# A gated mix of linear attention and a squared-ReLU MLP: TensorE's order written by hand, operands of 448 columns moved to another place in their 256 bytes

## The chip, the cores and the metric

The kernel runs on one core of a Trainium2 chip. The metric is the device time of one launch in microseconds. All matrix products take float32 data in the float32r form, and most numbers are split in two parts (`h` and `l`, for high and low), so that one logical product of two split operands is three matmuls: high by high, high by low, low by high.

## What is computed

```python
x = A_x                                       # 2048 x 448, float32
g = sigmoid((x * gate_w).sum(-1))             # one gate for each row
# a: linear attention, 16 heads of 28
q, k, v = split(x @ A_wqkv)
phi = lambda t: where(t > 0, t + 1, exp(t)) + 1e-6
kv  = einsum("hsd,hse->hde", phi(k), v);  z = phi(k).sum over s
o   = (phi(q) @ kv) / (phi(q) . z + 1e-6)
a   = o @ A_wo
# b: MLP, 448 -> 1792 -> 448
b   = relu(x @ B_w1 + B_b1) ** 2 @ B_w2 + B_b2
return g * a + (1 - g) * b
```

## The kernel before

The 2048 rows are cut into four blocks `b` of 512 columns of the transposed `x` (`xt`), and each block into four tiles `t` of 128 rows. The 448 input features are four chunks `c`; the last one is packed so that two matmuls do for it, and a product over all features is 11 matmuls (3 + 3 + 3 + 2). The 1792 hidden features are 14 slices `f` of 128.

`up(b, f)` makes one hidden slice: 11 matmuls with moving operands of 512 columns into `h_ps` (line 213), then ReLU and square on ScalarE (lines 217, 218) and the split on VectorE (`hh`, `hl`; lines 62, 65). `down(b, f)` multiplies it with `w2` into four accumulators `o_ps`: 12 matmuls whose moving operand has 448 columns (line 242). `keys(t)` is 11 matmuls with the key weights `wk_s` as moving operand. In this kernel that operand has 450 columns: the two last ones carry the gate's weights, and a one-column copy (line 280) takes the gate's logit out of `k_ps`. `gram(b, c)` accumulates phi(k) by x (`g_ps`, 12 matmuls of 448 columns, 8 for the last chunk).

There are two stages. In the first, each block does hidden slices 0 to 6, its keys and its gram. In the second, the blocks come in the order 3, 0, 1, 2 (`order`; `n` counts the place in it, `fl` the slice in the half) and do slices 7 to 13, the queries (`q_ps`, 11 matmuls of 512 columns, 7 for `c == 3`), the denominators (`d_ps`), the scaling of the queries (`scaled`: `qh`, `ql`) and the attention (`a_ps`, 11 matmuls of 448 columns for a tile). `finish` joins the two results and stores a tile.

At the seam between the stages stands the product of kv with the output weights. `kv_product` (`kv_ps`, line 364) is followed by four `m_product(j)`, of three matmuls each, into `m_ps`. Each result is split into the tile `m`, of which there is one buffer (`tag="m", bufs=1`), and spread over the partitions of `m_s` by five DMAs that GpSimd issues (lines 398 to 400). `m_ps` shares two PSUM buffers (`ms_p`, tag `ms`) with `k_ps`, `g_ps`, `q_ps`, `d_ps` and `a_ps`, in the order in which the source asks for them.

A planner (`TileContext`) orders the instructions of every engine by its own estimates: the order of the source is a priority, and TensorE's blocks may be cut into each other. Around the slices 9 and 10 of a block in the second stage, for instance, it laid the matmuls of `a_ps`, `h_ps` and `o_ps` between each other. Semaphores keep the data right whatever the order; each engine runs its own list strictly in order.

Matmul operands lie in SBUF at addresses that the pools assign. In this kernel's program the moving operands of 512 columns begin at a multiple of 256 bytes in their partition, those of 448 and 450 columns at 64 modulo 256, but for the 12 of `m_ps`, which begin at 0 modulo 256. Small unused ends of tiles (`warm`, `side`, `off`, `wkm`, the 16 columns behind `w1`) set these places.

At the start, `load_w1(0, 0, c)` and `load_x(0, c)` alternate on SyncE's queue, with the first x chunk in two halves; 18 warm-up matmuls on zeros run meanwhile, and `up_chunk` then works chunk by chunk over four hidden slices.

Of the kernel before, what the change touches and what calls it, by code (L numbers as in the profile page):

```python
# [15 lines left out]
P = 128  # L16
# [14 lines left out]
def gated_mix_kernel(ctx: ExitStack, tc: tile.TileContext, xt, xn, wk, wq, wv, wo, w1a, w1b, w2, b1, b2, hmask,  # L31
# [4 lines left out]
    keep = ctx.enter_context(tc.tile_pool(name="keep", bufs=1))  # L36

# [59 lines left out]
    def load_x(b, c, a=0, z=TB):  # L97
        if a == 0:
            x_raw[b, c] = slot([P, TB], F, f"xr{b}_{c}")
        load(x_raw[b, c][:, a:z], xt[b, c][:, a:z])  # L100

    def split_x(b, c, a=0, z=TB):
        if c == 0 and a == 0:
            xs[b] = (keep.tile([P, 4, TB], R, name=f"xh{b}", tag="xh", bufs=2),
                     keep.tile([P, 4, TB], R, name=f"xl{b}", tag="xl", bufs=2))
        (xh, xl), r = xs[b], x_raw[b, c]
        if c < 3:
            split_hi(act, xh[:, c, a:z], r[:, a:z])
            split_lo(dve, xl[:, c, a:z], r[:, a:z], xh[:, c, a:z])
        else:  # L110
            split_last(xh[:, 3, a:z], xl[:, 3, a:z], r[:, a:z], side)
# [11 lines left out]
    def load_w1(h, g, c):  # L123
        w1_raw[h, g, c] = slot([P, (TB, 3 * P)[g]], F, f"w1r{h}{g}{c}")
        load(w1_raw[h, g, c], (w1a, w1b)[g][h, c])

    def split_w1(h, g, c, hi_eng=act):
        if c == 0:
            n = (TB, 3 * P)[g]
            w = keep.tile([P, 7 * n + (16, 0)[g]], R, name=f"w1_{h}{g}", tag=f"w1{g}", bufs=1)  # L130
            w1_s[h, g] = w[:, :7 * n].rearrange("p (c n) -> p c n", c=7)
        split_w(w1_s[h, g], c, w1_raw.pop((h, g, c)), hi_eng, dve)
# [20 lines left out]
    def load_wk(c):  # L153
        wk_raw[c] = slot([P, D + 2], F, f"wkr{c}")
        load(wk_raw[c], wk[c])
# [4 lines left out]
    warm = keep.tile([P, 400], mybir.dt.bfloat16, name="warm")[:, :256]  # L160
    dve.memset(warm, 0.0)
    warm_ps = acc_p.tile([P, 512], F, name="warm_ps", tag="acc")
    for _ in range(18):
        pe.matmul(warm_ps[:, :256], warm[:, :P], warm, start=True, stop=True)
# [6 lines left out]
    for c in range(4):  # L171
        load_w1(0, 0, c)
        if c == 0:
            load_x(0, c, 0, TB // 2)
            load_x(0, c, TB // 2, TB)
        else:
            load_x(0, c)
# [12 lines left out]
    b2_s = keep.tile([P, D], F, name="b2_s")  # L190
    hm = keep.tile([P, P], R, name="hm")
    dve.memset(ones, 1.0)
    ksum = keep.tile([P, D], F, name="ksum")
    part = [keep.tile([P, D], F, name=f"part{t}") for t in range(NT)]
# [8 lines left out]
    def up_chunk(ps, b, f, c):  # L203
# [8 lines left out]
        for n, (a, m) in enumerate(terms):  # L212
            pe.matmul(ps, a, m, start=(c == 0 and n == 0), stop=(c == 3 and n == 1))  # L213

    def hidden(ps, b, f):
        r = slot([P, TB], F, f"hr{b}_{f}")
        act.activation(r, ps, AF.Relu, bias=b1_s[:, f:f + 1])  # L217
        act.activation(r, r, AF.Square)  # L218
        h = slot([P, TB], R, f"hh{b}_{f}")
        lo = slot([P, TB], R, f"hl{b}_{f}")  # L220
        split_hi(dve, h, r)
        split_lo(dve, lo, r, h)
        hs[f] = (h, lo)

    def up(b, f):
# [3 lines left out]
        hidden(ps, b, f)  # L229
# [34 lines left out]
    def keys(t):  # L264
        b, i = divmod(t, 4)
        ps = ms_p.tile([P, 512], F, name=f"k_ps{t}", tag="ms")
        products(ps[:, :D + 2], [term for c in range(4)
                                 for term in terms_x(*xs[b], slice(i * P, (i + 1) * P), wk_s, slice(0, D + 2), c)])
# [6 lines left out]
        if t == 0:  # L275
            pool.memset(tmp_p.tile([P, 48], F, name="off"), 0.0)

        def after():
            phi(ps[:, :D], e, r, p)
            dve.tensor_copy(logit[:, t:t + 1], ps[:, D:D + 1])  # L280
# [8 lines left out]
            raw = xn_raw.pop(t)  # L289
            split_hi(act, nh[:, :D], raw)  # L290
# [22 lines left out]
    wq_s = keep.tile([P, 7, TB], R, name="wq_s")  # L313
# [72 lines left out]
    def m_product(j):  # L386
# [5 lines left out]
        def after():  # L392
# [4 lines left out]
            for c in range(3):  # L397
                pool.dma_start(out=m_s[p:p + 32, c::4, :D][:, :2], in_=m[c * 32:c * 32 + 32])
            pool.dma_start(out=m_s[p:p + 16, 3, :D], in_=m[96:112, 0])
            pool.dma_start(out=m_s[p + 16:p + 32, 3, :D], in_=m[112:, 1])  # L400
# [67 lines left out]
    def attention(b, i):  # L468
# [4 lines left out]
        for c in range(3):  # L473
            h, lo = qs[c]
            terms += [(h[:, cols], m_s[:, c, :D]), (h[:, cols], m_s[:, 4 + c, :D]), (lo[:, cols], m_s[:, c, :D])]
        h, lo = qs[3]
        terms += [(h[:, cols], m_s[:, 3, :D]), (lo[:, cols], m_s[:, 3, :D])]
# [4 lines left out]

    todo = []
# [10 lines left out]
    for c in range(4):  # L494
        if c == 0:
            split_x(0, 0, 0, TB // 2)
            split_w1(0, 0, 0, hi_eng=dve)
            split_x(0, 0, TB // 2, TB)
# [3 lines left out]
        for f in range(4):  # L502
            up_chunk(first[f], 0, f, c)
    for f in range(2):
        hidden(first[f], 0, f)
# [5 lines left out]
    wkm = keep.tile([P, 3632], R, name="wk_s", tag="wkm", bufs=1)  # L511
    wk_s = wkm[:, :7 * TB].rearrange("p (c n) -> p c n", c=7)
# [4 lines left out]
    for c in range(4):  # L517
        split_w(wk_s[:, :, :D + 2], c, wk_raw[c], act, dve)
# [5 lines left out]
    split_w2(2)  # L524
    load(b2_s, b2.partition_broadcast(P))
# [31 lines left out]
    todo += gram(0, 0)  # L557
    split_x(1, 2)
    down(0, 5)
    run_todo()  # L560
    todo += gram(0, 1)
    split_x(1, 3)

    for b in range(1, NB):
        for f in range(NH):
            run_todo()
            up(b, f)
            if f == 0:
                down(b - 1, NH - 1)
                half_done(b - 1)  # L570
                if b == 1:
                    todo += gram(0, 2)
                    run_todo()
                    todo += gram(0, 3)
                    run_todo()
# [48 lines left out]
    for n, b in enumerate(order):  # L624
        then = order[n + 1] if n + 1 < NB else None
        for f in range(NF - NH, NF):
            fl = f - NH
            run_todo()
            up(b, f)
# [6 lines left out]
            else:  # L636
                down(order[n - 1], NF - 1)
                for i in range(4):
# [113 lines left out]
```

## Time and profile before

| | us |
|---|---|
| median of 3 runs | 442.17 (442.09 to 443.4) |
| the profiled execution | 441.92 |
| its span, first to last instruction | 440.1 |
| TensorE busy | 432.9 |
| VectorE busy | 268.0 |
| ScalarE busy | 172.7 |
| GpSimd busy | 58.5 |

The span is the time between the first and the last instruction that the profiler saw; the execution's own time is 1.8 us longer. A busy TensorE is one with a matmul in flight: the matmuls of a row overlap, so the time that a matmul costs is read from the distance of two starts, not from its length. Times in the rows are microseconds from the start of the span. In a row of the timeline the bracket is the idle time before it and what ended it.

### The profile page before, as it was taken

Reading aid. Unit: us, or ns where it says so; the run is one execution under the profiler, and the core shown is the slowest. Engines: PE = TensorE matmul, PEld = TensorE weight load, DVE = VectorE, ACT = ScalarE, POOL = GpSimd, SP = SyncE. Lnnn points to the kernel's source line nnn. Section 1 sums busy time; section 2 is a strip of 40 time slices with the busy share of each in tenths; the row PEclk is TensorE's granted clock in tenths of the full one; section 3 lists DMA queues with packets and bytes.
Section 4 is the critical chain, followed back from the end, with each engine's and each line's share of the span. In section 5 each row is a group of like instructions: output and inputs, shape, how many; then the busy total and the mean of one; then the engine's idle time right before and its main releaser. Section 6 shows DMA issues by size and latency. Waiting matters only on the chain.

```text
span 440.1 us, 5482 instructions
## 1 busy us (share of the span) xinstructions
PE 432.9 (98%) x2054; PEld 380.7 (87%) x2054; DVE 268.0 (61%) x452; ACT 172.7 (39%) x298; POOL 58.5 (13%) x76
## 2 busy tenths in 40 slices
PE   9999999999999999999999989999999999999996
PEld 6798898899888889898988868888888898888895
DVE  5958436552587427573467668788454984549423
ACT  5955235331355114451344334335322453234321
POOL 0233124210252005420002420000000000000000
PEclk9999999999999999999999999999999999999999
DMA  7652201021031210333146311040100501002002
GB/s 264 188 174 69 89 13 57 24 66 47 24 118 31 67 45 1 110 102 82 54 123 151 73 38 24 1 147 33 25 0 0 181 0 26 0 0 85 1 1 83
DMA packets 18315, 28.77 MB, mean 65 GB/s; under 512 B 2880, under 2 KB 12784, under 8 KB 18288
## 3 DMA queue, kind: packets, MB, share of 16 engines
q1 hardware_dynamic: 17072, 26.81, 19.9%
q0 software_dynamic: 1216, 1.61, 1.9%
q8 instruction: 16, 0.26, 0.3%
q14 instruction: 11, 0.09, 0.1%
HBM read 22.09 MB, written 3.67 MB: 59 GB/s over the span
## 4 chain that ended last, share of the span: by engine, by line
PE 91%; DVE 3%; DMA 2%; ACT 2%; issue 1%; SPq 0%; DVEq 0%; ACTq 0%
PE o_ps L242 30%; PE h_ps L213 28%; PE q_ps L77 8%; PE a_ps L77 8%; PE g_ps L77 8%; PE k_ps L77 7%; DMA wkr<-in_wk 1%; DMA xr<-in_xt 1%; PE kv_ps L364 1%; ACT hr L217 1%; PE m_ps L77 1%; DVE wk_s L65 0%; DVE hh L62 0%; DVE r L261 0%; DVE r L262 0%
## 5 line engine op out<-in xcount | busy, mean ns | idle before, releaser
L213 PE MATMUL h_ps<-xh,w 128*128 128x512 f32 x392 | 126.9, 392 | 0.1
L242 PE MATMUL o_ps<-w,hh 128*128 128x448 f32 x448 | 125.5, 363 | 0.7 <-DVE hh L62 0.7
L242 PEld LDWEIGHTS o_ps<-w,hh 128*128 128x128 f32 x448 | 83.8, 188 | 10.2 <-DVE hh L62 1.4
L213 PE MATMUL h_ps<-xl,w 128*128 128x512 f32 x224 | 87.5, 391 | 0.0
L213 PEld LDWEIGHTS h_ps<-xh,w 128*128 128x128 f32 x392 | 73.5, 188 | 15.4 <-ACT xh L58 0.4
L242 PE MATMUL o_ps<-w,hl 128*128 128x448 f32 x224 | 79.6, 363 | 0.0
L217 ACT ACTIVATE hr<-h_ps,b_s 128x512 f32<-128x512 f32 x56 | 38.3, 683 | 96.9 <-PE h_ps L213 89.8
L62 DVE CAST hh<-hr 128x512 fp32r<-128x512 f32 x56 | 25.3, 452 | 40.4 <-ACT hr L218 40.0
L213 PEld LDWEIGHTS h_ps<-xl,w 128*128 128x128 f32 x224 | 42.1, 188 | 8.3 <-DVE xl L65 0.4
L242 PEld LDWEIGHTS o_ps<-w,hl 128*128 128x128 f32 x224 | 42.0, 188 | 2.9 <-DVE hl L65 0.2
L65 DVE TENSOR_TENSOR hl<-hr,hh 128x512 fp32r<-128x512 f32 x56 | 41.1, 734 | 2.2
L218 ACT ACTIVATE hr<-hr 128x512 f32<-128x512 f32 x56 | 35.3, 630 | 1.3
L77 PE MATMUL k_ps<-wk_s,xh 128*128 128x450 f32 x112 | 33.7, 367 | 0.0
L77 PE MATMUL q_ps<-xh,wq_s 128*128 128x512 f32 x100 | 33.0, 390 | 0.0
L77 PE MATMUL a_ps<-m_s,qh 128*128 128x448 f32 x112 | 32.2, 362 | 0.0
L65 POOL TENSOR_TENSOR nl<-xnr,nh 128x384 fp32r<-128x384 f32 x16 | 18.2, 1139 | 94.2 <-ACT nh L58 94.2
L286 POOL TENSOR_TENSOR ksum<-ksum,r 128x448 f32<-128x448 f32 x15 | 19.3, 1284 | 52.1 <-DVE r L262 52.1
L481 DVE SCALAR_TENSOR_TENSOR part<-part,gate,u 128x448 f32<-128x448 f32 x16 | 10.9, 683 | 24.9 <-ACT u L480 24.9
L480 ACT ACTIVATE u<-a_ps,gate 128x448 f32<-128x448 f32 x16 | 10.2, 635 | 37.2 <-PE a_ps L77 37.2
L261 DVE TENSOR_SCALAR r<-k_ps 128x448 f32<-128x448 f32 x16 | 10.0, 623 | 23.7 <-ACT e L260 21.7
L77 PE MATMUL k_ps<-wk_s,xl 128*128 128x450 f32 x64 | 23.6, 369 | 0.0
L77 PE MATMUL g_ps<-pl,nh 128*128 128x448 f32 x64 | 23.3, 364 | 0.3 <-DVE pl L65 0.3
(104 smaller groups left out, 562.0 us busy)
## 6 DMA issues: line engine op xcount, KB each, us to landing
xr<-in_xt SPq DMA_DIRECT2D x27, 256.0 KB, 3.2
xnr<-in_xn SPq DMA_DIRECT2D x16, 224.0 KB, 2.6
out<-out SPq DMA_DIRECT2D x16, 224.0 KB, 2.0
w2r<-in_w SPq DMA_DIRECT2D x14, 224.0 KB, 2.9
w1r<-in_w1a SPq DMA_DIRECT2D x8, 256.0 KB, 2.8
w1r<-in_w1b SPq DMA_DIRECT2D x8, 192.0 KB, 2.9
m_s<-m POOLq DMA_DIRECT2D x12, 112.0 KB, 2.7
wqr<-in_wq SPq DMA_DIRECT2D x4, 256.0 KB, 3.0
```

Source lines behind the costliest of these rows:

```text
L62: eng.tensor_copy(hi, src)
L65: eng.tensor_tensor(lo, src, f32(hi), op=ALU.subtract)
L77: pe.matmul(out_ps, a, b, start=(i == 0), stop=(i == n - 1))
L213: pe.matmul(ps, a, m, start=(c == 0 and n == 0), stop=(c == 3 and n == 1))
L217: act.activation(r, ps, AF.Relu, bias=b1_s[:, f:f + 1])
L218: act.activation(r, r, AF.Square)
L242: pe.matmul(o_ps[i][:, :D], a, m, start=(f % NH == 0 and n == 0), stop=(f % NH == NH - 1 and n == 2))
L261: dve.tensor_scalar(r, ps, 0.0, 1e-6, op0=ALU.max, op1=ALU.add)
L286: pool.tensor_tensor(ksum, ksum, p, op=ALU.add)
L364: pe.matmul(kv_ps[:JE, js], wv_s[c][:, js], gsum[c][:, js], start=(c == 0), stop=(c == 3))
L480: act.activation(u, ps[:, :D], AF.Copy, scale=gate[:, 0, t:t + 1])
L481: dve.scalar_tensor_tensor(part[t], part[t], gate[:, 1, t:t + 1], u, op0=ALU.mult, op1=ALU.add)
```

## The change

TensorE is put under `tc.manual_schedule`: its instructions stand in the order of the source, uncut. The planner goes on ordering the other engines. The source was rearranged for that at the seam (`m_product`, `split_wo`), at `gram` of block 0, at the attention of the first block of the second stage, and at the end. The attention of the other three blocks keeps its place: tile `i` at slice `fl == i + 2`.

```diff
+    ctx.enter_context(tc.manual_schedule(engines={pe.engine}))
     todo = []
...
     split_x(1, 1)
     split_w2(6)
-    todo += gram(0, 0)
     split_x(1, 2)
     down(0, 5)
-    run_todo()
-    todo += gram(0, 1)
+    todo += gram(0, 0)
     split_x(1, 3)
...
             run_todo()
-            up(b, f)
+            if n == 0 and fl in (1, 2):
+                split_wo(2 * fl - 2)
+                split_wo(2 * fl - 1)
+            up(b, f, 2 if then is None and f == NF - 1 else 1)
+            if n == 0 and fl in (1, 2):
+                todo += m_product(2 * fl - 2)
+                run_todo()
...
             else:
                 down(order[n - 1], NF - 1)
                 for i in range(4):
+                    if n == 1:
+                        attention(order[0], i)
                     finish(order[n - 1], i)
             if n == 0:
+                if fl in (1, 2):
+                    todo += m_product(2 * fl - 1)
+                    run_todo()
                 if fl < 4:
                     todo += queries(b, (3, 0, 1, 2)[fl])
...
-                if fl in (1, 2):
-                    for j in range(2 * fl - 2, 2 * fl):
-                        split_wo(j)
-                        todo += m_product(j)
...
-                if fl == 6:
-                    for i in range(4):
-                        attention(b, i)
...
     last = order[-1]
+    down(last, NF - 2, range(3))
     for i in range(4):
-        for f in (NF - 2, NF - 1):
-            down(last, f, [i])
+        if i == 3:
+            down(last, NF - 2, [i])
+        down(last, NF - 1, [i])
         finish(last, i)
```

In the built program TensorE's blocks then follow each other like this, at the seam and in the second block after it (11 `q_ps` matmuls are 7 for `q3_3`):

```
q3_3 kv h3_8 m0 d3_7 m1 q3_0 h3_9 m2 d3_8 m3 q3_1 h3_10 d3_9 q3_2 h3_11 d3_10 den3 h3_12 d3_11 ...
q1_2 h1_7 d0_13 den1 h1_8 d1_7 h1_9 d1_8 a4 h1_10 d1_9 a5 q2_3 h1_11 ...
```

(`h3_8` is `up(3, 8)`, `d3_7` is `down(3, 7)`, `den3` is `denominators(3)`, `a4` is the attention of tile 4.)

The places of the 448-column moving operands change from 64 to 160 modulo 256: 1,200 matmuls of `o_ps`, `a_ps`, `g_ps` and `k_ps`. Those of 512 columns and those of `m_ps` stay where they were, and so do the stationary operands, but for the mask of the denominators. The pads that do this (`w1`, `wq_s`, `off`, `warm` laid into `part[0]`, `wk_s` and `m_s` as plain tiles of 7 x 448):

```diff
+    def new_w1(h, g):
+        n, a, z = ((TB, 0, 40), (3 * P, 24, 0))[g]
+        w = keep.tile([P, a + 7 * n + z], R, name=f"w1_{h}{g}", tag=f"w1{g}", bufs=1)
...
-    wkm = keep.tile([P, 3632], R, name="wk_s", tag="wkm", bufs=1)
-    wk_s = wkm[:, :7 * TB].rearrange("p (c n) -> p c n", c=7)
+    wk_s = keep.tile([P, 7, D], R, name="wk_s", tag="wkm", bufs=1)
```

The keys have 448 columns, and the logit comes from a VectorE instruction over the row tile of x and a broadcast gate weight `gw_s`, which is one more DMA of 224 KB on SyncE's queue (source line behind `split_w2(2)`; in the built program it stands behind the key weights, ahead of `b2_s`):

```diff
-        products(ps[:, :D + 2], ...)
+        products(ps[:, :D], ...)
...
-            dve.tensor_copy(logit[:, t:t + 1], ps[:, D:D + 1])
...
+            dve.scalar_tensor_tensor(e, raw, 1.0, gw_s, op0=ALU.mult, op1=ALU.mult, accum_out=logit[:, t:t + 1])
```

At the start x is loaded ahead of w1, chunk by chunk; the first w1 chunk comes in halves instead of the first x chunk; there are 15 warm-up matmuls instead of 18; and the first chunk's 12 matmuls go term by term over the four slices instead of slice by slice. Slice 0 of block 0 and the very last hidden slice go through ReLU, square and split in two halves of 256 columns (`parts=2`):

```diff
     for c in range(4):
-        load_w1(0, 0, c)
+        load_x(0, c)
         if c == 0:
-            load_x(0, c, 0, TB // 2)
-            load_x(0, c, TB // 2, TB)
+            load_w1(0, 0, c, 0, TB // 2)
+            load_w1(0, 0, c, TB // 2, TB)
...
+        if c == 0:
+            for n in range(3):
+                for f in range(4):
+                    up_chunk(first[f], 0, f, c, n)
...
-    for f in range(2):
-        hidden(first[f], 0, f)
+    hidden(first[0], 0, 0, 2)
+    hidden(first[1], 0, 1)
```

In the built program VectorE takes the low part of the first w1 chunk ahead of the low part of the first x chunk.

133 lines of the change are left out of this document (73 added, 60 removed).

## The prediction

> **What bounds the kernel now.** First the page: who is busy, and the chain of work that ended last.
>
> ```profile
> span 440.1 us, 5482 instructions
> PE 432.9 (98%) x2054; PEld 380.7 (87%) x2054; DVE 268.0 (61%) x452; ACT 172.7 (39%) x298; POOL 58.5 (13%) x76
> ...
> PE 91%; DVE 3%; DMA 2%; ACT 2%; issue 1%; SPq 0%; DVEq 0%; ACTq 0%
> ```
>
> TensorE (PE) is the bound. So a change pays only if it makes matmuls closer to each other or closes a gap between them, and every new wait of TensorE is paid in full. The view of busy time by stretches says where gaps are:
>
> ```profile
> 50.00:216.00 166.00, 166.00 (x797) 148.82 (x796) 87.12 (x145) 58.15 (x104) 36.23 (x39) 1.00 0.20 59
> 262.00:436.00 174.00, 174.00 (x819) 153.25 (x818) 113.44 (x187) 63.11 (x102) 0.45 (x1) 1.00 0.11 35
> ```
>
> The second number is TensorE's busy time, the next ones those of its weight loads, VectorE, ScalarE and GpSimd: TensorE is without a gap from 50 to 216 and from 262 to 436. An order of one's own has nothing to win there; it can only lose. What there is to win stands in these rows of the timeline, with the wait in the bracket:
>
> ```profile
> 16.16 1.08 PE L242 MATMUL o_ps<-w,hh 128*128 128x448 f32 x4 [0.75 <-DVE hh L62]
> ...
> 47.44 0.48 PE L77 MATMUL g_ps<-ph,nh 128*128 128x448 f32 x1 [0.18 <-ACT ph L58]
> ...
> 48.60 0.47 PE L77 MATMUL g_ps<-pl,nh 128*128 128x448 f32 x1 [0.28 <-DVE pl L65]
> ...
> 258.44 0.50 PE L77 MATMUL d_ps<-dh,hm 128*128 128x512 f32 x1 [1.32 <-ACT dh L58]
> ...
> 259.36 0.39 PE L77 MATMUL d_ps<-dl,hm 128*128 128x512 f32 x1
> ```
>
> A bracket is short of the loss, because a matmul counts as busy for some 0.15 us after the next could start, and the matmul after a wait takes another 0.11. So the losses are 0.75 + 0.26 = 1.0 at 16, 0.18 + 0.28 + 0.52 = 1.0 at 47 to 49, and at 258 1.32 + 0.15 and the 0.92 from 258.44 to 259.36, in which only two matmuls of 0.23 start: 1.9.
>
> What a matmul costs comes from the chain of waits, whose pieces are (start, length, how many):
>
> ```profile
> 19.05 2.26 PE k_ps L77 x11
> ...
> 236.07 0.63 PE m_ps L77 x3
> ...
> 252.34 2.53 PE q_ps L77 x11
> ...
> 270.96 8.80 PE a_ps L77 x44
> 279.76 4.99 PE q_ps L77 x22
> ```
>
> `k_ps` (450 columns) takes 2.26 / 11 = 0.2055 us, `a_ps` (448 columns, 64 modulo 256) 8.80 / 44 = 0.200, and so do `o_ps` and `g_ps`, `m_ps` (448 columns, 0 modulo 256) 0.63 / 3 = 0.21, `q_ps` (512 columns, 0 modulo 256) 4.99 / 22 = 0.227.
>
> **Keys of 448 columns: -1.0.** 176 matmuls of `k_ps` go from 0.2055 to 0.200. The logit instead costs 16 VectorE instructions like `part` below for 16 small copies: 0.68 each, 11 us of VectorE in stage one, where it is busy 87 of 166 us (second fence). That is at nothing as long as TensorE does not wait for what stands behind it on VectorE, as it does not from 50 to 216; ahead of 50 it has a price (below).
>
> ```profile
> L481 DVE SCALAR_TENSOR_TENSOR part<-part,gate,u 128x448 f32<-128x448 f32 x16 | 10.9, 683 | 24.9 <-ACT u L480 24.9
> ```
>
> **The place of the 448-column operands: -2.4, ends -15 and +11.** 1,200 matmuls move from 64 to 160 modulo 256, and the trace has none at 160. The only other place that it shows is 0, with 0.21 instead of 0.200 (0.0095 before rounding): that end is 1,200 x 0.0095 = +11. For the other end I take what a column costs at the margin: 0.0268 from `a_ps` to `q_ps` for 64 columns more, 0.42 ns each, so that 448 columns without an overhead would take 0.1876, 0.0124 less than now, and 1,200 x 0.0124 = -15. No row lies between them. The nearest is no change (the same matmul 96 bytes away). From 0 to 64 the pitch fell by 0.01; I allow a fifth of that step once more, 2 ns, -2.4.
>
> The Trainium skill's page "SBUF — State Buffer" (Door 1, the note on cachelines) gives SBUF 16-byte lines; 64 and 160 are both multiples of 16, and by that the move would be worth nothing and the sum 2.4 higher. This trace does not bear it out: 0 is a multiple of 16 too and costs 0.01 more than 64.
>
> **Start and slice 0: -0.3 (-0.9 to +0.4).** Before, TensorE began at 5.0 us, when `xl` of the first x half was there:
>
> ```profile
> 1.06 3.99 PE L164 MATMUL warm_ps<-warm 128*128 128x256 bf16 x18 [1.06 <-DVE warm L161]
> 5.02 0.73 PE L213 MATMUL h_ps<-xh,w 128*128 128x512 f32 x2
> ...
> 4.48 0.94 DVE L65 TENSOR_TENSOR xl<-xr,xh 128x256 fp32r<-128x256 f32 x2
> ```
>
> Now four matmuls (high by high) can begin when the 15 warm-up ones end, 1.06 + 15 x 3.99 / 18 = 4.4. Four of the other eight need all of `xl`, which VectorE makes behind both w1 halves and behind the low part of w1 (0.69, like `ql` further down, of the same size). I take the second w1 half to land as late as the second x half before, about 4.5, and 0.25 for its cast: 4.8 + 0.69 + 0.94 = 6.4, and eight matmuls from then end at 6.4 + 8 x 0.228 = 8.2. Before, all twelve followed from 5.02 and ended at about 5.02 + 0.15 + 12 x 0.228 = 7.9: +0.3. Halves for slice 0 bring its first `hh` forward by about 0.6 of the 1.0 lost at 16.
>
> **Fixed order, first block: -0.3.** `gram(0, 0)` now follows a complete `down(0, 5)`, 2.4 us of work that hides the 1.0 at 47 (-1.0). But `up(0, 4)` is no longer cut open. Before, the planner had put other matmuls between its parts while its weights were split; the last of those splits ends at 28.25:
>
> ```profile
> 26.98 1.27 DVE L65 TENSOR_TENSOR w<-w1r,w 64x384 fp32r<-64x384 f32 x1
> ```
>
> In the new order TensorE stands at the last chunk of `up(0, 4)` at about 27.3, and a logit instruction of 0.68 comes ahead of the split: +0.7 (0.4 to 1.1).
>
> **Fixed order at the seam: +3.5 (1.5 to 5).** `m1` may be written only when the five DMAs of `m0` have read it. ScalarE's reads of `m_ps` show that turn:
>
> ```profile
> 241.55 0.55 ACT L58 ACTIVATE m<-m_ps 128x448 fp32r<-128x448 f32 x1 [0.71 <-DMA m_s<-m]
> ...
> 247.35 0.55 ACT L58 ACTIVATE m<-m_ps 128x448 fp32r<-128x448 f32 x1 [1.06 <-DMA m_s<-m]
> ```
>
> 5.8 us from one to the next, with a wait for the DMAs ahead of each, and I allow one more. Now count from the end of h8 in the new order. `m0`, d7, `m1`, q3_0, h9 take 0.6 + 2.4 + 0.6 + 2.5 + 2.5, so `m2` is due at 8.6. ScalarE reads `m0` at about 2.1, behind h8's ReLU and two instructions of 0.6, so it can read `m1` 5.8 to 6.8 later, at 7.9 to 8.9. `m2` needs the PSUM buffer of `m1`, read by ScalarE and then VectorE (0.55 + 0.65), and behind that on VectorE two instructions (0.7 + 0.6) of which the second makes the low part of `wo` for `m2`: it starts at 10.4 to 11.4, and TensorE waits 1.8 to 2.8; I take 2.5. q3_1 takes the buffer of `m2`, whose read waits for `m1`'s DMAs: 1.0 more. Queued behind ScalarE's wait are its reads of q3_0 and the `wo` splits, which is part of this.
>
> **`den3` is placed later: -1.9.** It follows q3_2 by h11 and d10, 2.5 + 2.4 = 4.9 us. Before, q3_2 ended at 254.87 (last row of the chain above) and the operand `dl` of its last matmul was there at 259.36, 4.5 later. So the loss at 258 goes.
>
> **Attention in fixed order: +7.7 (5 to 9).** The matmuls of `a4` end with `qh` and `ql` of chunk 3. This is the second block, as it ran, TensorE by the chain, VectorE by the timeline:
>
> ```profile
> 342.85 2.51 PE h_ps L213 x11
> 345.36 2.41 PE o_ps L242 x12
> 347.76 4.79 PE h_ps L213 x21
> 352.55 2.41 PE o_ps L242 x12
> ...
> 346.46 3.38 DVE L453 RECIPROCAL rec<-rec 128x128 f32<-128x128 f32 x4
> ...
> 357.05 0.68 DVE L65 TENSOR_TENSOR ql<-qe,qh 128x512 fp32r<-128x512 f32 x1
> ```
>
> The x21 is h9 with ten matmuls of h10 pulled ahead of d8: the planner kept TensorE busy while VectorE, which had the reciprocals from 346.46 and nothing but work from there, made `ql`. Uncut, h8, d7, h9, d8 and the first nine of `a4` end at 342.85 + 2.5 + 2.4 + 2.5 + 2.4 + 2.2 = 354.9 with the two that need chunk 3 still to come, but `ql` is there at 357.7 and its matmul ends at 358.0: 3.1 late. VectorE's list in the changed program has the same order there, so nothing comes sooner. In the third block VectorE has no x chunks to split for a next one, so I take a little less, 2.7. First block (`a12` to `a15` now stand ahead of `den0`): from the end of `a15` VectorE needs u, part and finish (2.0, three like `part` above), the reciprocals (3.38) with their sums (0.65) and what came between them and `ql` here (349.8 to 357.7, 8.0), together 14.0; TensorE has 12.0 and `den0`'s 0.5; +0.3 for the last matmul: 1.9. In each, h10 and the rest only shift.
>
> **End: -0.2.** The last slice in halves takes most of 0.3 us of waits near 433.
>
> **Sum**, against the profiled execution's 441.92 (its span 440.1 and 1.8 around it; the median of the runs is 0.25 above): -1.0 - 2.4 - 0.3 - 0.3 + 3.5 - 1.9 + 7.7 - 0.2 = +5.1, so 447.0, and for a median 447.2.
>
> **Rivals.** (1) *The new place takes most of a matmul's overhead away.* At 0.189, nine tenths of the way from 0.200 to the end of 0.1876, the 1,200 matmuls give -13; the waits on VectorE grow by what TensorE comes sooner (35 such matmuls in each of three blocks and some at the seam, 0.011 each, about +1.5): the sum without its -2.4 is 449.6, and 449.6 - 13 + 1.5 = 438.1. It decides from 7 ns a matmul on. For it: 64 against 0 shows that the place matters; against: 512 and 448 columns now have the same overhead, about 0.012 by the margin above, as if at a floor. Chance 0.24. The Trainium skill's page "TensorE: Matmul & The Clock Gate" (Back-to-back issue gap) has columns / 2.4 GHz + 2.5 ns, which is 189 ns for 448 columns and would make this rival the outcome; this trace's 200 does not agree with it so far. (2) *The waits at seam and attention do not come*, because the other engines get their lists early enough: 447.2 less the 3.5 and the 7.7 is 436.0. Against: VectorE had nothing but work from 346.46 to 357.7. 0.08. (3) *The place is worse*, as at 0: 449.6 + 11 = 460, slower still; it decides against rivals 1 and 2 from 0.007 a matmul on. 0.08. (4) My forecast: 0.60, of it 0.05 within 0.3% of before, where the place gives about 6 ns.
>
> **Numbers.** 0.3%, 1.3 us, is about what a measurement of this kernel can tell from no change. Faster: rivals 1 and 2, 0.32. Same: 0.05. Slower: 0.63. The forecast's own range is 442 to 452. To leave out no more than 2 in 10 the range goes down to 436, past the middle of rival 1, and up to 453.
>
> **What would show it.** Right: brackets at `a0`, `a4`, `a8` naming VectorE's `qh` and `ql`, 2 to 3 us a block; at `m2` naming `wol` or `m`, and at q3_1; none at `den3` and none at `g_ps` of block 0; `k_ps` at 0.200 like the others. Wrong: a pitch of `o_ps` below 0.193, or 262 to the end without a gap on TensorE.

## The result, and the profile after

The changed kernel takes 455.61 us (median of 6 runs, 454.75 to 457.01), the kernel before 442.13 beside it. The ratio is 1.0304, with an interval of 1.0283 to 1.0324: 3% slower, where 447.2 and at most 453 were forecast. The profiled execution took 456.44, its span is 454.7, 14.6 more than before. Its page, first the busy times, then the chain that ended last:

```profile
span 454.7 us, 5518 instructions
PE 438.2 (96%) x2051; PEld 381.0 (84%) x2051; DVE 282.8 (62%) x473; ACT 172.7 (38%) x301; POOL 63.4 (14%) x76
...
PE 78%; DVE 13%; DMA 2%; issue 2%; ACT 2%; SPq 2%; DVEq 0%; ACTq 0%
```

TensorE had 91% of the chain and has 78%; VectorE went from 3% to 13%. So TensorE now waits for VectorE. Where, the view by stretches tells (TensorE is the second number, the granted clock the one behind GpSimd's):

```profile
50.00:216.00 166.00, 166.00 (x798) 148.78 (x797) 97.18 (x159) 58.67 (x105) 39.18 (x39) 1.00 0.20 58
216.00:250.00 34.00, 29.33 (x149) 24.56 (x148) 22.16 (x41) 14.67 (x28) 8.21 (x15) 1.00 0.44 112
250.00:262.00 12.00, 12.00 (x57) 10.39 (x56) 6.95 (x13) 4.20 (x7) 2.60 (x5) 1.00 0.16 33
262.00:330.00 68.00, 66.53 (x310) 57.86 (x310) 49.31 (x80) 26.73 (x44) 0.00 (x0) 1.00 0.12 37
330.00:436.00 106.00, 101.97 (x462) 86.87 (x461) 60.67 (x100) 33.77 (x55) 0.00 (x0) 0.98 0.09 30
```

Nothing is lost from 50 to 216, though VectorE does 10 us more there: the logit is hidden. The gap at `den3` is gone (250 to 262). New gaps stand at the seam and in the attention, and from 330 on the granted clock is 0.98. These are the waits in TensorE's timeline:

```profile
28.15 0.50 PE L223 MATMUL h_ps<-xh,w 128*128 128x512 f32 x1 [0.83 <-DVE w L66]
28.83 0.47 PE L223 MATMUL h_ps<-xh,w 128*128 128x512 f32 x1 [0.18 <-DVE w L66]
...
238.50 0.44 PE L78 MATMUL m_ps<-woh,kv_h 112*128 112x448 f32 x1 [1.97 <-ACT w L59]
239.53 0.47 PE L78 MATMUL m_ps<-wol,kv_h 112*128 112x448 f32 x1 [0.59 <-DVE wol L66]
...
245.21 0.50 PE L78 MATMUL q_ps<-xh,wq_s 128*128 128x512 f32 x1 [1.92 <-DVE m L66]
...
306.69 0.47 PE L78 MATMUL a_ps<-m_s,qh 128*128 128x448 f32 x1 [1.00 <-DVE qh L72]
...
357.52 0.47 PE L254 MATMUL o_ps<-w,hl 128*128 128x448 f32 x1 [0.52 <-DVE hl L66]
...
363.00 0.47 PE L78 MATMUL a_ps<-m_s,qh 128*128 128x448 f32 x1 [1.40 <-DVE qh L72]
363.93 0.47 PE L78 MATMUL a_ps<-m_s,ql 128*128 128x448 f32 x1 [0.47 <-DVE ql L66]
364.24 0.45 PE L223 MATMUL h_ps<-xh,w 128*128 128x512 f32 x1
364.49 0.63 PE L223 MATMUL h_ps<-xl,w 128*128 128x512 f32 x1
364.92 1.05 PE L223 MATMUL h_ps<-xh,w 128*128 128x512 f32 x2
...
420.60 0.47 PE L78 MATMUL a_ps<-m_s,qh 128*128 128x448 f32 x1 [0.80 <-DVE qh L72]
```

From start to start, against the distance of two undisturbed starts, the losses are 1.5 at `up(0, 4)`, 3.1 at `m2`, 2.2 at q3_1, 0.5 at `m0`; 2.0 at `a0`; 0.9 at d1_8 and 2.4 at `a4`; 0.9 and 1.9 at d2_8 and `a8`. The three rows from 364.24 on show something else: behind `a4` no wait is left, yet a matmul of 512 columns starts 0.43 after the one ahead of it (364.49 to 364.92) instead of 0.227. The view by stretches around it shows the granted clock there:

```profile
355.00:360.00 5.00, 4.48 (x21) 3.52 (x20) 5.00 (x10) 3.88 (x8) 0.00 (x0) 1.00 0.46 166
360.00:364.00 4.00, 2.13 (x10) 1.40 (x9) 4.00 (x8) 1.79 (x4) 0.00 (x0) 1.00 0.00 0
364.00:368.00 4.00, 4.00 (x11) 3.16 (x12) 3.12 (x5) 0.64 (x1) 0.00 (x0) 0.57 0.00 0
368.00:372.00 4.00, 4.00 (x22) 3.67 (x21) 1.12 (x2) 1.32 (x2) 0.00 (x0) 1.00 0.00 0
```

The granted clock is 0.57 for these 4 us, behind 4 us in which TensorE was busy 2.13: eight matmuls at half the clock, 1.6 lost. At undisturbed places the matmuls cost this (the chain of waits; at the end of the row the count):

```profile
69.55 2.20 PE k_ps L78 x11
71.75 2.52 PE h_ps L223 x11
74.27 2.43 PE o_ps L254 x12
...
284.74 8.81 PE a_ps L78 x44
```

`k_ps` costs 0.200, as forecast. `a_ps` stays at 0.200, but evenly: before, the distances were spread over 0.197 to 0.202, now all but a few are 0.200. `o_ps` got dearer: over all its starts 0.2024 instead of 0.2008.

### The profile page after: what moved, and what is told of

Same layout as the page of the kernel before. It is cut to its first block, busy times and chain, and to the rows that moved or that the text cites. A ratio compares the mean times of both kernels' runs of the same rounds, so it can differ in the third digit from the quotient of the medians.

```text
span 454.7 us, 5518 instructions
## 1 busy us (share of the span) xinstructions
PE 438.2 (96%) x2051; PEld 381.0 (84%) x2051; DVE 282.8 (62%) x473; ACT 172.7 (38%) x301; POOL 63.4 (14%) x76
## 4 chain that ended last, share of the span: by engine, by line
PE 78%; DVE 13%; DMA 2%; issue 2%; ACT 2%; SPq 2%; DVEq 0%; ACTq 0%
PE o_ps L254 25%; PE h_ps L223 23%; PE g_ps L78 8%; PE q_ps L78 8%; PE k_ps L78 7%; PE a_ps L78 7%; DVE rec L466 2%; DVE ql L66 2%; SPq L52 2%; DVE qe L474 1%; DVE out L264 1%; DMA w1r<-in_w1a 1%; DVE hl L66 1%; DMA b_s<-in_b 1%; PE kv_ps L377 1%
## 5 line engine op out<-in xcount | busy, mean ns | idle before, releaser
L254 PE MATMUL o_ps<-w,hl 128*128 128x448 f32 x224 | 81.9, 365 | 1.0 <-DVE hl L66 1.0
L231 ACT ACTIVATE hr<-h_ps,b_s 128x512 f32<-128x512 f32 (+1 forms) x58 | 38.6, 669 | 108.4 <-PE h_ps L223 97.7
L63 DVE CAST hh<-hr 128x512 fp32r<-128x512 f32 (+1 forms) x58 | 25.6, 441 | 48.7 <-ACT hr L232 48.3
L66 DVE TENSOR_TENSOR hl<-hr,hh 128x512 fp32r<-128x512 f32 (+1 forms) x58 | 40.5, 699 | 2.7
L232 ACT ACTIVATE hr<-hr 128x512 f32<-128x512 f32 (+1 forms) x58 | 35.5, 616 | 1.5
L78 PE MATMUL k_ps<-wk_s,xh 128*128 128x448 f32 x112 | 32.8, 362 | 0.0
L297 POOL TENSOR_TENSOR ksum<-ksum,r 128x448 f32<-128x448 f32 x15 | 22.8, 1518 | 47.4 <-DVE r L274 42.0
L78 PEld LDWEIGHTS a_ps<-m_s,qh 128*128 128x128 f32 x112 | 21.0, 188 | 5.5 <-DVE qh L72 4.1
L78 PE MATMUL a_ps<-m_s,ql 128*128 128x448 f32 x64 | 23.6, 369 | 1.3 <-DVE ql L66 1.2
L78 PEld LDWEIGHTS q_ps<-xh,wq_s 128*128 128x128 f32 x100 | 18.8, 188 | 6.0 <-DVE m L66 2.3
```

Source lines behind the costliest of these rows:

```text
L63: eng.tensor_copy(hi, src)
L66: eng.tensor_tensor(lo, src, f32(hi), op=ALU.subtract)
L78: pe.matmul(out_ps, a, b, start=(i == 0), stop=(i == n - 1))
L231: act.activation(r[:, c], ps[:, c], AF.Relu, bias=b1_s[:, f:f + 1])
L232: act.activation(r[:, c], r[:, c], AF.Square)
L254: pe.matmul(o_ps[i][:, :D], a, m, start=(f % NH == 0 and n == 0), stop=(f % NH == NH - 1 and n == 2))
```

## The experiments

Each is a small edit of the changed kernel, unless it says otherwise. A median stands beside the kernel before on the same chip, 442.3 to 442.4 in all four sets, and beside 455.6 for the changed kernel, which was timed once, for the result above.

**The planner orders TensorE again.**

```diff
-    ctx.enter_context(tc.manual_schedule(engines={pe.engine}))
```

> The changed kernel without the manual order: the planner orders TensorE again, everything else (rearranged source, keys of 448 columns, logit on VectorE, places at 160, the new start) stays. Theory (the waits come from the fixed order): the waits at m2 and q3_1 (3.1 + 2.2), a0 (2.0), a4 (2.4 and 1.6 of half clock behind it), a8 (1.9), d1_8 and d2_8 (0.9 each) and up(0, 4) (1.5) go or shrink to those of the kernel before; keys -0.9, pitches of o_ps and q_ps +1.4: 442 (440 to 444). Rival (the VectorE work of the logit, the places or the rearranged source cost most of it): 448 or more.

445.69 (443.75 to 447.68), ratio 1.0070 (1.0046 to 1.0094). So the hand-written order is some 10 of the 13.5 us. But a kernel with the rest of the change is still slower than before. In its profile no wait over 0.1 is left between 262 and the end, but a wait at `m2` has stayed:

```profile
242.60 0.47 PE L78 MATMUL m_ps<-woh,kv_h 112*128 112x448 f32 x1 [2.18 <-ACT woh L59]
243.44 0.47 PE L78 MATMUL m_ps<-wol,kv_h 112*128 112x448 f32 x1 [0.37 <-DVE wol L66]
```

**The attention one slice later.**

```diff
-                if 2 <= fl < 6:
-                    attention(b, fl - 2)
+                if 3 <= fl < 7:
+                    attention(b, fl - 3)
```

> The changed kernel with the attention of tile i one slice later (slice i + 3 instead of i + 2) in the three last blocks. Theory (TensorE comes to a0, a4, a8 before VectorE's chain of reciprocals and scalings has made qh and ql, by 1.9 to 2.4 us, and the half clock at 364 follows from that wait): 4.9 us more of matmuls stand ahead, the three waits go, the clock does not drop: -2.0 - 2.4 - 1.6 - 1.9, 447.7 (446.5 to 449). The 0.9 at d1_8 and d2_8 stay. Rival (VectorE is short of time as a whole, the wait comes back at a later place): 452 or more.

453.32, ratio 1.0237 (1.0201 to 1.0274): 2.3 won instead of 7.9. The rival's number came true and the waits came back later; its reason, that VectorE is short of time as a whole, did not hold (the run with more cover, below). The waits at `a0`, `a4` and `a8` are gone, and the first two have come back a slice later, ahead of d9:

```profile
363.63 0.68 PE L254 MATMUL o_ps<-w,hh 128*128 128x448 f32 x2 [0.96 <-DVE hh L63]
364.83 0.47 PE L254 MATMUL o_ps<-w,hl 128*128 128x448 f32 x1 [0.53 <-DVE hl L66]
```

VectorE's list has `hh` and `hl` of h9 between the scalings, one ahead of chunk 3's `ql` and one behind it. So `down` hangs on the same chain as the attention, and cover ahead of the attention alone doesn't help it.

**A second buffer for `m`.**

```diff
-        m = late.tile([P, 2, D], R, name=f"m{j}", tag="m", bufs=1)
+        m = late.tile([P, 2, D], R, name=f"m{j}", tag="m", bufs=2)
...
-    NSLOT, NLATE = 15, 15
+    NSLOT, NLATE = 15, 14
```

> The changed kernel with two buffers for m (and 14 instead of 15 buffers for the late tiles, to make room). Theory A (m1 can't be written before m0's five DMAs have read m0): ScalarE reads m1 some 6 us earlier, the waits of TensorE at m2 (3.1) go and that at q3_1 (2.2) falls below 1: 451 (450 to 452.5). Theory B (ScalarE's list has the exponential of q3_3 ahead of m1's read, and that waits until 235.9 for the DMAs that exchange the halves of q3_3): m1's read stays at 236.5, the wait at m2 stays, at q3_1 at most 1 is won: 454.6 to 455.6.

453.62, ratio 1.0237 (1.0197 to 1.0278). Half of each theory: `m1` is read early, and TensorE waits at `m2` all the same. ScalarE's timeline, first of the changed kernel, then with two buffers:

```profile
229.16 0.54 ACT L59 ACTIVATE m<-m_ps 128x448 fp32r<-128x448 f32 x1
...
235.94 0.63 ACT L272 ACTIVATE qe<-qv 128x512 f32<-128x512 f32 x1 [5.20 <-DVE qv L453]
236.47 0.53 ACT L59 ACTIVATE m<-m_ps 128x448 fp32r<-128x448 f32 x1
```

```profile
231.74 0.54 ACT L59 ACTIVATE m<-m_ps 128x448 fp32r<-128x448 f32 x1 [0.94 <-PE m_ps L78]
236.28 0.63 ACT L272 ACTIVATE qe<-qv 128x512 f32<-128x512 f32 x1 [4.00 <-DVE qv L453]
236.82 0.58 ACT L272 ACTIVATE qe<-q_ps 128x512 f32<-128x512 f32 x1
237.29 0.57 ACT L59 ACTIVATE woh<-wor 112x448 fp32r<-112x448 f32 x1
```

The read of `m1` comes 4.7 us earlier. But `woh` for `m2` stands in ScalarE's list behind the exponential of q3_3 (`qe<-qv`), and that waits for the exchange of q3_3's halves, eight DMAs behind each other on SyncE's queue. The load of that `wo` stands behind the same eight DMAs: it is issued at 231.97 and lands at 236.5, 0.8 before its split begins. Of the 3.1 at `m2` 2.7 remain, now named `woh` and `wol`. The 2.2 at q3_1 is gone.

**Back to 64 modulo 256.**

```diff
-        n, a, z = ((TB, 0, 40), (3 * P, 24, 0))[g]
+        n, a, z = ((TB, 0, 16), (3 * P, 48, 0))[g]
```

> The changed kernel with the moving operands of o_ps, a_ps and k_ps back at 64 modulo 256 (two unused ends: 16 columns instead of 40 behind the first w1 tile, 48 instead of 24 ahead of the second); g_ps stays at 160 as a control. Theory (the place sets the pitch: 160 makes o_ps dearer, 202.4 instead of 200.75 ns, and makes a_ps, g_ps and k_ps even at 200.0): o_ps at 200.75, a_ps and k_ps spread over 197 to 202 with the same mean, g_ps even at 200: -1.1, 454.5. Rival (o_ps is dearer for another reason, the order or the traffic beside it): o_ps stays at 202.4, time as it is, 455.6.

454.87, ratio 1.0268 (1.0233 to 1.0302). `o_ps` is back at 0.2007 and `a_ps` and `k_ps` are spread over 0.197 to 0.202 again; `g_ps`, left at 160, is not as even as it was (0.2010). The 512-column matmuls, whose place did not change, became cheaper too, `q_ps` from 0.2292 to 0.2277 and `h_ps` from 0.2287 to 0.2277. By these distances the place is worth 1.7 us. The medians differ by 0.7, which this experiment can't separate from the spread of a kernel with so many waits. So the same was asked of the quieter kernel before:

**The kernel before with `o_ps`, `a_ps` and `k_ps` at 160.**

```diff
-            w = keep.tile([P, 7 * n + (16, 0)[g]], R, name=f"w1_{h}{g}", tag=f"w1{g}", bufs=1)
-            w1_s[h, g] = w[:, :7 * n].rearrange("p (c n) -> p c n", c=7)
+            a = (0, 24)[g]
+            w = keep.tile([P, a + 7 * n + (40, 0)[g]], R, name=f"w1_{h}{g}", tag=f"w1{g}", bufs=1)
+            w1_s[h, g] = w[:, a:a + 7 * n].rearrange("p (c n) -> p c n", c=7)
...
-    wkm = keep.tile([P, 3632], R, name="wk_s", tag="wkm", bufs=1)
+    wkm = keep.tile([P, 3584], R, name="wk_s", tag="wkm", bufs=1)
...
-                    m_s = keep.tile([P, 3632], R, name="m_s", tag="wkm", bufs=1)
+                    m_s = keep.tile([P, 3584], R, name="m_s", tag="wkm", bufs=1)
```

> The kernel before with one thing changed: the moving operands of o_ps, a_ps and k_ps at 160 instead of 64 modulo 256 (g_ps stays at 64, instruction lists as they were). Theory (160 makes o_ps 1.7 ns dearer and the 512-column matmuls 1 to 1.5 ns, and evens a_ps out at 200): 672 x 1.7 + 616 x 1 + 160 x 1.5 ns = +2.0 on the kernel before, 444.3 (443.5 to 445). Rival (the dearer pitch comes from the other parts of the change): no difference, 442.4.

444.19 (443.48 to 446.31), ratio 1.0041 (1.0027 to 1.0055): +1.9, as the distances had it. The place costs time: in the kernel before by the medians, in the changed kernel by the distances alone. The chain shows `o_ps` at 2.43 for twelve, where the kernel before has 2.41:

```profile
69.66 2.43 PE o_ps L243 x12
72.09 2.27 PE k_ps L77 x11
```

**Take-up of q3_3 one step later, and `down(0, 2)` first.** With two buffers for `m` as above.

```diff
-            return [join]
+            return [lambda: [join]]
...
-    up(0, 4)
-    run_todo()
     down(0, 2)
+    up(0, 4)
+    run_todo()
```

> The changed kernel with two edits at separate places. Seam: two buffers for m as in the run before, and the exchanged halves of q3_3 are taken up one slice later, so that ScalarE's and VectorE's lists have the splits of wo for m2 ahead of them. First block: down(0, 2) ahead of up(0, 4). Theory (at m2 TensorE waits for the wo splits, which stand behind q3_3's exponential, which waits for the exchange; up(0, 4) waits for the split of its weights): the waits at m2 (3.1), q3_1 (2.2) and up(0, 4) (1.5) all go, no half clock at 240: 449 (448 to 450.5). Rival (the wo splits are late because their loads are, or VectorE's list is too long there): 1.5 or more stays at m2, 451 or more.

456.55, ratio 1.0318 (1.0305 to 1.0332). A miss in two ways. At the seam the edit did not do what it was meant for: the pending steps are run more than once in that slice, so the take-up still stands ahead of the `wo` splits, and `m2` waits 2.5. In the first block the 1.5 at `up(0, 4)` is gone, but the time was not won: `a0` waits more, and its profile has half clock at three places, where the changed kernel's has it at one. All four of its runs have a mean granted clock of 0.987 to 0.992, the changed kernel's six have 0.994 to 0.996.

**Idle time filled with useless matmuls.** They go into the PSUM tile of the next hidden slice, which overwrites them.

```diff
+    early = {}
+
+    def h_tile(b, f):
+        return mm_p.tile([P, 512], F, name=f"h_ps{b}_{f}", tag="mm")
...
-        ps = mm_p.tile([P, 512], F, name=f"h_ps{b}_{f}", tag="mm")
+        ps = early.pop((b, f)) if (b, f) in early else h_tile(b, f)
...
+        for n, (a, m) in enumerate(terms):
+            if i == 0 and b < NB - 1 and n > 8:
+                if n == 9:
+                    early[b, NF - 4] = h_tile(b, NF - 4)
+                for _ in range((5, 7, 5)[b] if n == 9 else 3):
+                    pe.matmul(early[b, NF - 4][:, :D], *terms[0], start=True, stop=True)
+            pe.matmul(ps[:, :D], a, m, start=(n == 0), stop=(n == 10))
-        products(ps[:, :D], terms)
```

> The changed kernel with idle TensorE time filled: 26 matmuls of 448 columns whose result nothing uses, 5, 7 and 5 ahead of the last but one matmul of a0, a4, a8 and 3 ahead of the last one, where TensorE waits 1.2, 1.6, 1.1 and 0.7. Theory (the half clock that follows for 3.4 us behind a4 comes from the idle time itself): the operands come no later, the waits are spent on useless work, and no matmul behind a4 takes 0.427: -1.6 in the executions that had it, 454.0 (453.5 to 454.6), with a smaller spread. Rival (the clock drops for another reason, or at a fixed time): the matmuls at 364 take 0.427 as before, 455.6 or up to 0.5 more.

455.55, ratio 1.0306 (1.0287 to 1.0324). In the profile the theory holds at `a4`: its last two matmuls start 5.5 and 6.4 behind the wait at d1_8, as in the changed kernel, and the matmuls behind them start 0.227 apart at full clock:

```profile
360.00:364.00 4.00, 4.00 (x21) 3.33 (x20) 4.00 (x8) 2.14 (x4) 0.00 (x0) 1.00 0.00 0
364.00:368.00 4.00, 4.00 (x19) 3.23 (x18) 3.58 (x6) 1.20 (x2) 0.00 (x0) 1.00 0.00 0
```

The median doesn't show the 1.6. In this profile the clock dropped behind the wait at `m2`, where it had not in the changed kernel's, and there it cost nothing: q3_1, which stands behind it, lost 0.7 instead of 2.2.

**The `wo` splits a slice earlier.** All four `wo` are loaded in the first slice and split ahead of `up(3, 8)`, with two buffers for `m`.

```diff
-            if n == 0 and fl in (1, 2):
-                split_wo(2 * fl - 2)
-                split_wo(2 * fl - 1)
+            if n == 0 and fl == 1:
+                for j in range(4):
+                    split_wo(j)
...
-                    for j in range(2):
+                    for j in range(4):
                         load_wo(j)
...
-                if fl == 1:
-                    for j in range(2, 4):
-                        load_wo(j)
```

> The changed kernel with two buffers for m, and all four wo loaded and split a slice earlier, ahead of the exchange of q3_3 in SyncE's queue and ahead of its take-up in ScalarE's and VectorE's lists. Theory (with m's second buffer, m2 waits for nothing but the wo splits behind that exchange): no wait at m2 and q3_1 (3.1 and 2.2 in the changed kernel, 2.5 and a half clock with two buffers alone): 450.5 (449.5 to 452). Rival (the PSUM buffer or the planner's lists put another wait there): 2 or more stays, 452.5 or more.

453.96, ratio 1.0253 (1.0234 to 1.0273). `m2` no longer waits and q3_1 waits no more than 0.1: the theory holds for both. The rival holds too: part of the win comes back earlier, at `m1` and q3_0, whose operands and buffer now stand behind the splits that were moved forward:

```profile
232.28 0.47 PE L78 MATMUL m_ps<-wol,kv_h 112*128 112x448 f32 x1 [0.32 <-DVE wol L66]
...
233.95 0.50 PE L78 MATMUL q_ps<-xh,wq_s 128*128 128x512 f32 x1 [1.00 <-DVE m L66]
```

Of 5.7 at the seam 2.9 are left. By the median this is no faster than two buffers alone (453.62).

**Low parts of x on GpSimd.**

```diff
-    def split_x(b, c):
+    def split_x(b, c, lo=dve):
...
-            split_lo(dve, xl[:, c], r, xh[:, c])
+            split_lo(lo, xl[:, c], r, xh[:, c])
...
-                    split_x(then, 2 * fl - 2)
-                    split_x(then, 2 * fl - 1)
+                    split_x(then, 2 * fl - 2, pool if n else dve)
+                    split_x(then, 2 * fl - 1, pool if n else dve)
```

> The changed kernel with the low parts of the next block's x, three chunks of four, made by GpSimd instead of VectorE in the three last blocks' turns that have a next one (1.3 us of the VectorE chain ahead of qh of chunk 3 in the second block, as much in the first, none in the third). Theory (the length of VectorE's chain sets when a0 and a4 go on): the waits at a0 and a4 get 1.2 shorter each, the one at a8 stays; with a shorter wait the half clock behind a4 is less likely: 453.2 (451.5 to 454). Rival (ScalarE or the reciprocals alone hold chunk 3, or GpSimd slows VectorE): a0 and a4 as they were, 455.6.

465.46, ratio 1.0524 (1.0496 to 1.0552), the slowest of all. While GpSimd works on an `xl`, a multiplication on VectorE takes 1.77 instead of 0.69. VectorE's timeline, then GpSimd's:

```profile
300.37 1.77 DVE L474 TENSOR_TENSOR qe<-rec,qe 128x512 f32<-128x512 f32 x1
302.07 0.68 DVE L66 TENSOR_TENSOR hl<-hr,hh 128x512 fp32r<-128x512 f32 x1
```

```profile
298.87 2.72 POOL L66 TENSOR_TENSOR xl<-xr,xh 128x512 fp32r<-128x512 f32 x2 [42.44 <-ACT xh L59]
```

So VectorE's chain got longer, not shorter, and `a0` waits 3.4 instead of 2.0, d1_8 and `a4` together 5.0 instead of 3.3, with half clock behind `a0` and behind d1_8. This profile is of the fastest of the four runs (462.24, mean clock 0.992); the others have 0.980 to 0.987, and what they lost beyond it no profile shows. That is the theory's sign with the opposite edit: what lengthens VectorE's chain is paid at `a0` and `a4`.

**More cover for both.** In the three last blocks `down` follows `up` by two slices from slice 10 on, and the attention comes a slice later. So h9 and h10 stand ahead of d8 and `a4`.

```diff
-                if n + 1 < NB or f + 1 < NF:
+                if n == 0 or fl == 1:
                     down(b, f - 1)
+                elif fl > 2:
+                    down(b, f - 2)
...
+                if n > 1:
+                    down(order[n - 1], NF - 2)
                 down(order[n - 1], NF - 1)
...
-                if 2 <= fl < 6:
-                    attention(b, fl - 2)
+                if 3 <= fl < 7:
+                    attention(b, fl - 3)
```

> The changed kernel with down two slices behind up instead of one, from slice 10 on in the three last blocks of the second stage, and the attention of tile i at slice i + 3: h9, h10 stand ahead of d8 and a0 (a4, a8). Theory (order: VectorE's chain of reciprocals, scalings and hidden splits lasts 14 us, and TensorE needs 4.9 us more cover for both its consumers, the attention and down): no wait at d8, d9, a0, a4, a8 and no half clock behind them: 455.6 - 8.1 - 1.6 = 446 (445 to 447.5). Rival (VectorE lacks time): the waits come back at a later place, 450 or more.

447.24, ratio 1.0110 (1.0083 to 1.0138), in the range of the theory. From 262 to 436 TensorE has no gap and the full clock:

```profile
262.00:330.00 68.00, 68.00 (x319) 59.55 (x318) 50.60 (x83) 26.96 (x45) 0.00 (x0) 1.00 0.12 37
330.00:436.00 106.00, 106.00 (x499) 93.36 (x498) 62.47 (x104) 36.67 (x61) 0.00 (x0) 1.00 0.09 31
```

VectorE has time enough (62.5 of 106). It was the order.

**All of it at once, under the hand order:** this, 64 modulo 256, two buffers for `m`, the earlier `wo`, `down(0, 2)` first.

> All causes found taken away under the hand order: as e14, and the operands at 64 modulo 256 (-1.9), two buffers for m and wo loaded and split a slice earlier (-2.9 of 5.7 at the seam), down(0, 2) ahead of up(0, 4) (-1.5). Theory (these terms are the whole loss and add up): 446 - 1.9 - 2.9 - 1.5 = 439.7 (438.5 to 441.5), no slower than the kernel before. Rival (a cause is missing): 443 or more.

441.30 (440.68 to 443.14), ratio 0.9974 (0.9957 to 0.9991). The causes found make up the whole loss: without them the hand order is no slower than the kernel before. It is not faster than the planner's versions below either.

**Versions for the planner.** First: planner, 64 modulo 256, two buffers for `m`.

> The changed kernel under the planner, with o_ps, a_ps and k_ps at 64 modulo 256 and two buffers for m: what is left is the keys of 448 columns, the logit on VectorE, the new start, the rearranged seam. Theory (place and order cost, the rest gains): against the planner's run at 445.7, -1.9 by the pitches and -3.7 by the waits at m2, which wait there for m0's DMAs: 440 (438.5 to 441.5), under the kernel before. Rival (the wait at m2 is then that for the wo splits, as with the manual order): 443 or more.

439.83 (439.46 to 440.62), ratio 0.9945 (0.9933 to 0.9956): the fastest version, 2.5 us under the kernel before. Then the same with the seam's source and the one buffer of the kernel before:

> The changed kernel under the planner at 64 modulo 256, and with the seam's source as it was in the kernel before (wo splits and m_product behind the queries of the slice, one buffer for m). Theory: no wait at m2, but one at den3 as in the kernel before (1.9) or none; keys -0.9, start and block 0 -0.6: 440.5 (439 to 442). Rival (the planner finds another order that waits at the seam again): 443 or more.

440.94, ratio 0.9976 (0.9963 to 0.9989), with the 1.9 at `den3` that the kernel before has. And the first with the earlier `wo`:

> The version that combines what the runs so far favour: the changed kernel under the planner, o_ps, a_ps and k_ps at 64 modulo 256, two buffers for m, and wo loaded and split a slice earlier. The same without the earlier wo took 439.8 and lost 1.4 at 241.8 behind m3 and 0.3 at den3. Theory (these hang on the wo splits too): 438.5 (437.8 to 439.3). Rival (the earlier loads push the x loads back): 440 or more.

440.75, ratio 0.9961 (0.9947 to 0.9976). In its profile the waits from 216 on are about 0.6 smaller than in the first version's, and the two profiled executions differ by 0.5 that way (440.14 and 440.60), yet its median is 0.9 higher; why stays open.

## Why the prediction was wrong

The direction was right and most of the steps, the size was not: +5.0 was forecast, +13.5 measured. By its own steps, with what the profile after has:

| step | forecast | measured |
|---|---|---|
| keys of 448 columns | -1.0 | -0.9 |
| place at 160 | -2.4 | +1.5 by the distances, +1.9 by itself |
| start and slice 0 | -0.3 | -0.2 |
| first block | -0.3 | +0.5 (up(0, 4) 1.5, gram 0) |
| seam | +3.5 | +5.7 |
| `den3` | -1.9 | -1.9 |
| attention | +7.7 | +8.1 |
| half clock | not named | +1.6 |
| end | -0.2 | -0.2 |

Together the right column is +14.2 (with the 1.5), of the 14.6 by which the spans differ.

*The attention* was right in mechanism, place and size: 2.0, 3.3 and 2.8 where 1.9, 3.1 and 2.7 stood. The brackets name `qh` and `ql`, as said, and the run with more cover takes all of it away. One part of it I had inside the sum without seeing it: 0.9 of the 3.3 is lost at d1_8, which waits for `hl` on the same chain. The run with the attention alone moved failed for that reason.

*The place* was mis-signed. The step took a fifth of the fall from 0 to 64 "once more", a trend drawn through two points, and one of them was misread: the row of 0.63 for three `m_ps` holds one distance of 0.228, while the other eleven in that trace are 0.201 to 0.212, in the middle 0.203. So 0 cost nearer 0.003 than 0.01 more than 64. The run on the kernel before shows +1.9 for the move to 160. The rival that the new place is worse was the right side, at a sixth of its size. The 16-byte lines of the Trainium skill's page "SBUF — State Buffer" (Door 1), from which the prediction took that two multiples of 16 cost the same, do not tell these places apart: 160 and 64 differ by 1.6 ns a matmul in `o_ps`. The rule of the Trainium skill's page "TensorE: Matmul & The Clock Gate" (Back-to-back issue gap) is not borne out either: 448 columns cost 0.200 or more in the mean at 0, 64 and 160, not 0.189.

*The seam* was under-sized. The step let `m2` wait for `m0`'s DMAs, then for the PSUM buffer and a split behind it. It missed the exchange of q3_3: the splits of `wo` stand behind it in ScalarE's and VectorE's lists, and their loads in SyncE's queue. With the DMAs of `m0` taken out of the way by the second buffer, 2.7 of 3.1 remained, and with loads and splits moved ahead of the exchange nothing. No run moves the splits alone; with two buffers the load would have held the split until 236.5, the list held it until 237.3. At q3_1 2.2 were lost instead of 1.0; VectorE's list there has five other instructions ahead of the low part of `m2` (it begins 1.6 us behind ScalarE's read).

*The first block* was under-sized by its own figures: with TensorE at 27.3 and the last split ending at 28.25, or 28.9 behind a logit instruction, the uncut `up(0, 4)` had to wait 1.6; the step counted the logit alone. In the changed kernel TensorE is due at 27.2, the last split ends at 28.68, and 1.5 are lost. The logit instruction was also dearer than the 0.68 of `part`: this form, which also sums along the row, takes 0.98, and 0.08 more to read the sum. Rows of VectorE's timeline of the changed kernel:

```profile
25.29 0.98 DVE L301 SCALAR_TENSOR_TENSOR e<-xnr,gw_s 128x448 f32<-128x448 f32 x1
26.20 0.08 DVE L301 DVE_READ_ACCUMULATOR e<-xnr,gw_s 128x1 f32 x1
...
26.73 1.95 DVE L66 TENSOR_TENSOR w<-w1r,w 128x384 fp32r<-128x384 f32 x2
```

*The half clock* was in no step. A wait was taken to cost its own length. In this kernel it can cost 1.6 more. All five profiles that have the changed kernel's wait at `a4` have half clock behind it, and the one with the wait filled has not: so far this part comes from the idle time. What it costs a whole run shows in the runs' mean granted clocks, which one such stretch lowers by 0.004: the planner's first run (the changed kernel under the planner) took 443.75 and 444.61 at 0.999 and 1.000, 447.42 and 447.61 at 0.991; with two buffers it was 452.79 and 453.00 at 0.999 and 0.998, 455.58 at 0.990. That is an estimated 1.2 to 1.5 us for each stretch, unless another wait stands behind the slow matmuls. Why the filling did not win as much is open: its one run at 1.000 took 455.05.

The largest part of the miss is the place (3.9 to 4.3), then the seam (2.2), the clock (1.6) and the first block (0.8).

## What to carry to other kernels

A planner that cuts one block's matmuls into another's does it to give the other engines time: whoever writes the order by hand must give that cover himself, and to every consumer of the late chain (here two slices ahead of `down` and the attention, not one ahead of the attention alone). Before a wait is put down to the DMA that it names, read what stands ahead in the list of the engine that makes the next operand: with the first hold gone, the second is there at once. A price taken from two points is no trend; a new place of operands is a thing to measure, and a pad of a few columns in the quiet kernel was enough to do so.

## What the runs showed of the hardware

*Place of a moving operand.* At 160 modulo 256, 448-column matmuls of `k_ps`, `g_ps` and `a_ps` start almost without exception 0.200 apart, at 64 they spread over 0.197 to 0.202 with the same mean. `o_ps` at 160 is spread the other way, 0.200 to 0.207, and costs 0.2024 instead of 0.2008. The 512-column matmuls of `q_ps`, which stay at 0, get 1.5 ns dearer beside them. The place of a matmul's own operand does not set its distance alone: `g_ps` at 160 goes from 0.2000 to 0.2010 when the others go to 64, and in the run with the attention later 22 of 176 `k_ps` take 0.206 or 0.207, though nothing in that edit changes their place. Why `o_ps` differs from `a_ps` was not found.

*The clock.* About 2 to 3 us of waiting within some 4 us can halve the granted clock for about 3.4 us (eight matmuls of 0.427), and need not: 2.5 to 3.1 us at `m2` did it in six of the profiles, and not in those of the changed kernel, of the planner's first run and of the run with GpSimd. The records of the granted clock show more: in all sixteen traces each stretch at full clock lasts a whole number of 3.413 us (the changed kernel's first one 358.40, 105 of them), so the clock drops only where such a period ends, counted from where it first went full. Every period in which no matmul was in flight for 1.84 us or more was followed by a drop, none with less than 1.6 was, and in between it went both ways. In the changed kernel the end of a period cuts the wait at `m2` in two, 1.63 and 0.94 (first two rows); the wait at `a4` lies within one, 1.87 (last two rows):

```profile
234.74:238.15 3.41, 1.78 (x8) 1.13 (x7) 2.63 (x5) 2.21 (x5) 0.63 (x1) 1.00 0.92 268
238.15:241.56 3.41, 2.47 (x11) 2.06 (x12) 3.41 (x7) 2.80 (x6) 2.09 (x4) 1.00 0.54 121
361.03:364.44 3.41, 1.54 (x6) 0.86 (x5) 3.41 (x8) 0.76 (x2) 0.00 (x0) 1.00 0.00 0
364.44:367.85 3.41, 3.41 (x9) 2.63 (x8) 2.68 (x5) 0.64 (x1) 0.00 (x0) 0.50 0.00 0
```

The Trainium skill's page "TensorE: Matmul & The Clock Gate" (What's actually happening) has a free-running window of 3.4 us and a drop after an idle one. The length agrees, and so does the chance in it; but here no period of 3.4 us inside a kernel had to be without matmuls, half of one was enough, and the longest single wait, in the run with GpSimd, was 2.9.

*GpSimd beside VectorE.* One subtraction on GpSimd with two operands in SBUF makes one VectorE instruction of 0.69 last 1.77 (rows above). The changed kernel has it too: the split at 26.73 lasts 1.36 beside one on GpSimd from 26.44 on, the same at 24.82 takes 0.55. The Trainium skill's page "SBUF — State Buffer" (Who interferes with whom) has VectorE's instructions with two inputs in SBUF contend with GpSimd's reads, the later one blocked; the rows agree.
